# Reciprocals behind the masks, w2 jobs four units sooner, and a last token tile in two halves, in a transformer block with linear attention and a Mish MLP

## The chip, the cores and the metric

The kernel runs on one core of a Trainium2 chip. The core has five engines, each with a queue of its own that it works through in order: TensorE (PE, matmuls and transposes; its weight loads are shown as PEld), VectorE (DVE), ScalarE (ACT), GpSimd (POOL) and SyncE (SP). SP, POOL and ACT issue transfers. The engines meet at semaphores. The metric is the device time in microseconds (us) of one execution; the time of the kernel before is the median of three runs.

## The reference

One block over 2048 tokens of width 512, in float32. The six modulation vectors come from one condition vector.

```python
mod = (silu(c) @ w_mod).reshape(1, 6, 1, 512)      # sa, ca, ga, sb, cb, gb
h = layernorm(x) * (1 + ca) + sa
x = x + ga * A(h)
h = layernorm(x) * (1 + cb) + sb
x = x + gb * B(h)

def A(h):                                          # linear attention, 32 heads of 16
    q, k, v = split_heads(h @ wqkv)
    phi = lambda t: where(t > 0, t + 1, exp(t)) + 1e-6
    pq, pk = phi(q), phi(k)
    kv = einsum("bhsd,bhse->bhde", pk, v)
    z = pk.sum over tokens
    o = (pq @ kv) / ((pq * z).sum(-1) + 1e-6)
    return merge_heads(o) @ wo

def B(h):                                          # 512 -> 1792 -> 512
    t = h @ w1 + b1
    return (t * tanh(softplus(t))) @ w2
```

## The kernel before

**Numbers.** Products are made to float32 accuracy from two faster ones: every operand is split into a high part of type float32r and a low part, the rest (`split`, L71: the high part on ACT or POOL at L75 or L77, the low part on DVE at L80). A product is three matmuls (`mm3`, L65): high by high (L67), high stationary by low streaming (L68), low stationary by high streaming (L69). The stationary operand is loaded for each matmul; the streaming one has 512 columns.

**Tiling.** Tokens stand in 4 blocks of 512 (`NB`), a block in 4 tiles of 128 rows. The inner width 1792 is 14 slices of 128 (`NF`). SBUF tiles of 128x512 come from one ring of 101 slots (`sb`); a tile that is taken later waits for the last reader of the slot. PSUM has four tiles tagged "acc", three tagged "h" and one tagged "tp" (`ps`).

**Order.** The order of every engine is the order in which the Python code issues; there is no scheduler. Main loops issue PE units one after the other, and generators spawned beside them (`spawn`) are moved one step at each `tick()`, in the order in which they were spawned. A generator's step so decides behind which other instructions of DVE, ACT, POOL or SP its own will stand. An engine that waits holds up all that is behind it in its queue.

**Stages.** First the k units and, over all tokens, the sums that the attention needs (to about 107 us of the span). Then `q_unit(b, g)` makes phi(q) for block 0 and 1; `kv_ps` (L746) and two masked copies on DVE (L749, "the masks") make the block diagonal state, and four matmuls `m_ps` fold wo into it. Then come q units of blocks 2 and 3 with the output units of block 0, and then the loop over blocks 1 to 3 in which `o_unit(b, t)` number n = 4b + t (n from 4 to 13) makes one token tile of the attention's output. Output units 14 and 15 follow the first products of the MLP.

**The denominators.** `attend(b, wait, queue)` (L593) makes them for block b: 16 small matmuls into a "tp" tile (L598) and, in its next step, on DVE the addition and the reciprocal (L602, L603, the tile `rden`). They go to DRAM (L605, `rden_d`), and four loads `rd` (L609) bring them back, each head's row spread over 16 partitions. After `wait` further steps DVE multiplies the four q tiles with them (L617), and they are split (tiles `qs`). Blocks 0 to 2 use POOL's queue, block 3 SP's. Block 0's matmuls are issued just ahead of `kv_ps`, and its other steps come at the ticks behind.

**w2.** `w2_job(f)` (L499) loads a slice of w2 (L501, `w2r`, on SP's queue), after two further steps multiplies it on DVE by gb (L504), splits it (`w_0h`, `w_0l`), and stores both parts to DRAM (L510, POOL). Jobs 0 and 1 are spawned in the loop of output units, the others later, in pairs. `w2_again` (L512) loads the parts back for later blocks.

**The MLP.** For blocks 0 and 1, and 2 and 3 together, the first product is a seven-product scheme over pairs of blocks and slices: `pair_first` and `pair_unit` (L846), with products of operands `t`, `b`, `a` and `s` in "h" or "tp" tiles (`p_a`, `p_s`) and sums on DVE (L836). Output units 14 and 15 (L629 adds them to the residual and so frees their "h" tiles) stand ahead of the first `pair_unit`. `d_unit(b, f)` (L809) adds slice f of the second product for one block to four "acc" tiles, one for each token tile; at the last slice DVE adds the residual (L819) and SP stores the token tile (L820). The last block's 14 d units are the end of the program, with nothing else on PE.

Of the kernel before, what the change touches and what calls it, by code (L numbers as in the profile page):

```python
# [11 lines left out]
ALU = mybir.AluOpType  # L12

P = 128
S = 2048
D = 512
F = 1792
NB = S // 512
NF = F // P
# [6 lines left out]
def block_kernel(ctx: ExitStack, tc: tile.TileContext, x, wqkv, wo, w1, b1t, w2, c, wmodt, out):  # L26
    nc = tc.nc
    act, dve, pool, pe, sp = nc.scalar, nc.vector, nc.gpsimd, nc.tensor, nc.sync
# [9 lines left out]
    def sb(name, dt=F32, shape=(P, 512)):  # L38

        return big.tile(list(shape), dt, tag="T", name=name, bufs=SLOTS)  # L40

    def ps(tag, name, shape=(P, 512)):
        return psp.tile(list(shape), F32, tag=tag, name=name, bufs=PBUFS[tag])
# [6 lines left out]
    def spawn(gen):  # L50
        fresh.append(gen)

    def tick():

        running.extend(fresh)
        fresh.clear()
        for g in list(running):
            if next(g, "end") == "end":
                running.remove(g)

    def run(gen):
        for _ in gen:
            pass

    def mm3(o, st, mv, start, stop):  # L65

        pe.matmul(o, st[0], mv[0], start=start, stop=False)  # L67
        pe.matmul(o, st[0], mv[1], start=False, stop=False)  # L68
        pe.matmul(o, st[1], mv[0], start=False, stop=stop)  # L69

    def split(name, t, keep, key, lo_engine=dve, hi_engine=act):  # L71

        hi, lo = sb(f"{name}h", F32R, t.shape), sb(f"{name}l", F32R, t.shape)
        if hi_engine is act:
            act.activation(hi, t, AF.Copy)  # L75
        else:
            hi_engine.tensor_copy(hi, t)  # L77
        if lo_engine is dve:
            yield
        lo_engine.tensor_tensor(lo, t, f32(hi), op=ALU.subtract)  # L80
        keep[key] = hi, lo


    xt, wm, wraw = {}, {}, {}

    def load_x(b, j, key="x", eng=sp):
        t = xt[key, b, j] = sb(f"{key}_{b}_{j}")
        r0 = 512 * b + P * j
        eng.dma_start(t, x[r0:r0 + P, :])
# [194 lines left out]
    def q_unit(b, g):  # L284
        p = ps("h", f"pq_{b}_{g}")
        gs = slice(P * g, P * (g + 1))
        for k in range(4):
            mm3(p, [w[:, gs] for w in wq[k]], hT["x", b, k], k == 0, k == 3)
        pq[b, g] = sb(f"q_{b}_{g}")
        spawn(phi(p, f"q_{b}_{g}", pq[b, g]))  # L290
# [101 lines left out]
    for k in range(4):  # L392
        hi, lo = sb(f"hT_x_0_{k}h", F32R), sb(f"hT_x_0_{k}l", F32R)
# [103 lines left out]
    w2s, w2d, op_a = {}, {}, {}  # L497

    def w2_job(f, wait=2):  # L499
        t = sb(f"w2r_{f}")  # L500
        sp.dma_start(t, w2[P * f:P * (f + 1), :])  # L501
        for _ in range(wait):
            yield
        dve.tensor_tensor(t, t, bc["gb"], op=ALU.mult)  # L504
        yield
        yield from split(f"w2_{f}", t, w2s, f)
        yield
        for i in range(2):
            w2d[f, i] = drp.tile([P, D], F32R, name=f"w2d_{f}_{i}")
            pool.dma_start(w2d[f, i], w2s[f][i])  # L510
# [82 lines left out]
    def attend(b, wait, queue=pool):  # L593

        p = ps("tp", f"den_{b}")[:, 0:P]
        for g in range(4):
            for t in range(4):
                pe.matmul(p[32 * t:32 * (t + 1), :], hmask[:, g, :], pq[b, g][:, P * t:P * (t + 1)],  # L598
                          start=g == 0, stop=g == 3)
        yield  # L600
        rden = cst.tile([P, P], F32, tag="rden", name=f"rden_{b}", bufs=2)
        dve.tensor_scalar(rden, p, TINY, 1.0, op0=ALU.add, op1=ALU.mult)  # L602
        dve.reciprocal(rden, rden)  # L603
        d = drp.tile([32, 512], F32, name=f"rden_d_{b}")
        queue.dma_start(bass.AP(tensor=d.tensor, offset=d.offset, ap=[[P, 4], [512, 32], [1, P]]), rden)  # L605
        rd = []
        for g in range(4):
            r = sb(f"rd_{b}_{g}")
            queue.dma_start(r, bass.AP(tensor=d.tensor, offset=d.offset + 8 * g * 512,  # L609
                                     ap=[[512, 8], [0, 16], [1, 512]]))  # L610
            rd.append(r)
        for _ in range(wait):
            yield
        parts = []
        for g in range(4):
            t = pq[b, g]
            dve.tensor_tensor(t, t, rd[g], op=ALU.mult)  # L617
            parts.append(split(f"qs_{b}_{g}", t, qs, (b, g)))
            next(parts[-1])
            if g % 2:  # L620
                yield
                run(parts.pop(0))
                run(parts.pop(0))
# [11 lines left out]
    def o_unit(b, t, tag="acc"):  # L635
        p = ps(tag, f"o_{b}_{t}")
        ts = slice(P * t, P * (t + 1))
        for g in range(4):
            mm3(p, [q[:, ts] for q in qs[b, g]], ms[g], g == 0, g == 3)
        spawn(o_post(p, b, t))  # L640
# [52 lines left out]
    def transpose_f(b, j, ptag="tp"):  # L693
        p = ps(ptag, f"tp_n_{b}_{j}")
        for t in range(4):
            pe.transpose(p[:, P * t:P * (t + 1)], xt["n", b, t][:, P * j:P * (j + 1)], ident)  # L696
        hf[b, j] = sb(f"hf_n_{b}_{j}")
        act.activation(hf[b, j], p, AF.Identity, bias=mc[:, 12 + j:13 + j], scale=mc[:, 16 + j:17 + j])  # L698

    def split_b(b, j, name):  # L700
        return split(f"{name}_{b}_{j}", hf[b, j], op_b, (name, j % 2))

    def columns(c0, c, done):

        b11, b12, b21, b22 = [hf.pop((b, c + h)) for h in (0, 2) for b in (c0, c0 + 1)]
        t = [sb(f"t_{c0}_{c}_{i}") for i in range(4)]
        for d, u, v in (t[0], b12, b11), (t[1], b22, t[0]), (t[2], b22, b12), (t[3], b21, t[1]):
            dve.tensor_tensor(d, u, v, op=ALU.subtract)
        yield
        names = [("b11", b11), ("t2", t[1]), ("t3", t[2]), ("t1", t[0]), ("b22", b22), ("t4", t[3]), ("b21", b21)]  # L710
        halves = [split(f"{name}_{c0}_{c}", v, op_b, (name, c)) for name, v in names if name not in done]
        for n in range(0, len(halves) + 2, 2):
            for h in halves[max(n - 2, 0):n] + halves[n:n + 2]:
                next(h, None)
            yield
# [19 lines left out]
    tick()  # L735
    run(early_rows[0])
    next(early_rows[1])
    attending = attend(0, 4)
    next(attending)
    spawn(attending)  # L740
    kv_ps = ps("acc", "kv_ps")
    for g in range(4):
        for k in range(4):
# [3 lines left out]
    for j in range(2):  # L747
        js = slice(64 * j, 64 * (j + 1))
        dve.tensor_tensor(kv.rearrange("p (g m) -> p g m", g=4)[js, :, js],  # L749
                          kv_ps.rearrange("p (g m) -> p g m", g=4)[js, :, js],  # L750
                          bmask[js, js].unsqueeze(1).to_broadcast([64, 4, 64]), op=ALU.mult)
    for g in range(1, 4):
        q_unit(1, g)
        load_x(2, g, "r")
        tick()
# [24 lines left out]
    for b in range(1, NB):  # L780
        for t in range(4):
            n = 4 * b + t
            for i, j in order.get(n, ()):
                transpose_f(i, j, "h")
                spawn(split_b(i, j, f"b{j // 2 + 1}{i + 1}"))
            if n in (12, 13):
                spawn(columns(0, n - 12, ("b11", "b12", "b21", "b22")))
            if n == 14:
                break
            o_unit(b, t)  # L790
            if b == 1:
                spawn(norm_each(1, t))
            if n == 5:
                spawn(attend(3, 3, sp))
            if n in (11, 12):
                spawn(w2_job(n - 11))
            tick()


    ag = {}  # L800
# [6 lines left out]
    oacc = {}  # L807

    def d_unit(b, f):  # L809
        if f == 0:  # L810
            for t in range(4):
                oacc[t] = ps("acc", f"oacc_{b}_{t}")
        for t in range(4):
            ts = slice(P * t, P * (t + 1))
            mm3(oacc[t], [a[:, ts] for a in ag[b, f]], w2s[f], f == 0, f == NF - 1)
            if f == NF - 1:
                v = xt["r", b, t]
                r0 = 512 * b + P * t
                dve.tensor_tensor(v, oacc[t], v, op=ALU.add)  # L819
                sp.dma_start(out[r0:r0 + P, :], v)  # L820

    ub = {}

# [50 lines left out]
    def second(b, side):  # L874

        for f in range(NF):
            side(f)
            ahead(b, f + NF)
            tick()
            d_unit(b, f)  # L880
# [34 lines left out]
    def trail(f):  # L915
        if tiles:
            spawn(tiles.pop(0))
        d_unit(0, f)
        ahead(1, f)
        tick()  # L920
# [64 lines left out]
```

## Time and profile before

| what | value |
|---|---|
| median of three runs | 504.95 us (504.88 to 506.96) |
| the profiled execution's own time | 506.47 us |
| its span, first to last instruction | 504.7 us |
| PE busy | 495.5 us (98%) |
| DVE busy | 360.3 us (71%) |
| ACT busy | 257.8 us (51%) |
| POOL busy | 112.9 us (22%) |
| moved by DMA | 77.29 MB, 153 GB/s on average |

Times in the views are microseconds from the span's start. A row of the view in order of time gives start, duration, engine, line, operation, the tile written and the tiles read (buffer numbers left out, so `t_0l` stands for several tiles), the shape, and in brackets how long the engine stood idle before it and what ended that. The record of a matmul also covers its way through the array, so consecutive records overlap: what counts is the step from start to start, 0.23 us for 512 columns. "SPq" rows are the issuing of a transfer, not its duration.

### The profile page before, as it was taken

The page shows a single profiled execution, that of the slowest core. Times are in us where ns is not written, and L with a number is a line of the kernel's source. Part 1 is how long each engine was busy: PE and PEld are TensorE (multiplying, and loading weights), DVE is VectorE, ACT ScalarE, POOL GpSimd, SP SyncE. Part 2 cuts the span into 40 slices and gives each one's busy share as a digit, 9 for nine tenths or more (in the row PEclk, how much of TensorE's full clock was granted, in tenths as well). Part 3 has the DMA queues.
Part 4 walks back from the last instruction along what each step waited for, and adds up shares of the span by engine and source line. Part 5 has one row for each costly group of instructions (what it writes and reads, how often), then busy time and mean ns, then how long its engine had stood idle before and what let it go on. Part 6 is the DMA issues. An engine that isn't in the chain of part 4 may idle for free.

```text
span 504.7 us, 6900 instructions
## 1 busy us (share of the span) xinstructions
PE 495.5 (98%) x2396; PEld 404.9 (80%) x2396; DVE 360.3 (71%) x707; ACT 257.8 (51%) x463; POOL 112.9 (22%) x204
## 2 busy tenths in 40 slices
PE   7999999999999999999999999999999999999996
PEld 5778888878778888878888888888888888888885
DVE  6889785889987978986987785359886556745302
ACT  6767573523351987836677765357253344445000
POOL 3480000100212311210233345421210111470000
PEclk9999999999999999999999999999999999999999
DMA  8821503472553315372565499982842445597002
GB/s 282 303 83 44 166 21 105 153 244 72 137 111 92 88 33 161 125 228 66 157 197 188 145 297 260 348 240 87 249 130 59 125 126 155 157 338 236 32 1 83
DMA packets 52233, 77.29 MB, mean 153 GB/s; under 512 B 5805, under 2 KB 20277, under 8 KB 52198
## 3 DMA queue, kind: packets, MB, share of 16 engines
q0 software_dynamic: 19600, 37.45, 25.6%
q1 hardware_dynamic: 32452, 39.14, 24.6%
q8 instruction: 19, 0.31, 0.2%
q10 hardware_dynamic: 146, 0.26, 0.1%
q14 instruction: 16, 0.13, 0.1%
HBM read 60.83 MB, written 15.99 MB: 152 GB/s over the span
## 4 chain that ended last, share of the span: by engine, by line
PE 84%; DVE 9%; DMA 4%; issue 1%; ACT 1%; POOL 1%; DVEq 0%; POOLq 0%; ACTq 0%
PE oacc L69 10%; PE oacc L67 10%; PE oacc L68 10%; PE p_s L67 5%; PE p_s L69 5%; PE p_s L68 5%; PE p_a L67 3%; PE p_a L69 3%; PE p_a L68 3%; DMA rd<-rden_d 3%; PE gacc L68 3%; PE gacc L69 3%; PE gacc L67 3%; PE pk L69 2%; PE pk L68 2%; PE pk L67 2%
## 5 line engine op out<-in xcount | busy, mean ns | idle before, releaser
L516 POOL DMA_DIRECT2D w2b<-w2d x84 | 44.9, 538 | 102.3 <-PE p_a L69 27.0
L827 ACT ACTIVATE ub<-c,b1c 128x512 f32<-128x512 f32 x28 | 19.0, 718 | 57.5 <-DVE c L836 53.8
L836 DVE TENSOR_TENSOR u<-p_s,u 128x512 f32<-128x512 f32 x28 | 19.4, 692 | 35.2 <-PE p_s L69 25.5
L819 DVE TENSOR_TENSOR rb<-oacc,rb 128x512 f32<-128x512 f32 x8 | 5.5, 692 | 32.9 <-PE oacc L69 32.9
L836 DVE TENSOR_TENSOR u<-p_a,u 128x512 f32<-128x512 f32 x26 | 17.6, 689 | 7.5 <-PE p_a L69 6.9
L698 ACT ACTIVATE hf_n<-tp_n,mc 128x512 f32<-128x512 f32 x16 | 11.7, 771 | 19.5 <-PE tp_n L696 19.5
L189 POOL TENSOR_TENSOR rs_n<-rs_n,half 128x1 f32<-128x1 f32 x16 | 9.4, 589 | 53.9 <-DVE rs_n L215 44.3
L804 ACT ACTIVATE u<-u,b1c 128x512 f32<-128x512 f32 x26 | 18.5, 712 | 2.6 <-DVE u L836 2.6
L836 DVE TENSOR_TENSOR c<-p_s,u 128x512 f32<-128x512 f32 x28 | 18.0, 683 | 1.9 <-PE p_s L69 1.3
L241 ACT ACTIVATE e_q<-pq 128x512 f32<-128x512 f32 x16 | 9.3, 588 | 18.4 <-PE pq L69 18.4
L853 ACT ACTIVATE u<-p_a 128x512 f32<-128x512 f32 x12 | 7.1, 588 | 18.7 <-PE p_a L69 18.7
L241 ACT ACTIVATE e_k<-pk 128x512 f32<-128x512 f32 x16 | 9.4, 591 | 13.3 <-PE pk L69 13.1
L617 DVE TENSOR_TENSOR q<-q,rd 128x512 f32<-128x512 f32 x16 | 10.7, 689 | 6.9 <-DMA rd<-rden_d 6.8
L189 POOL TENSOR_TENSOR rs_x<-rs_x,half 128x1 f32<-128x1 f32 (+1 forms) x10 | 7.1, 716 | 32.1 <-DVE rs_x L184 31.3
L243 DVE TENSOR_SCALAR e_k<-e_k 128x512 f32<-128x512 f32 x16 | 6.9, 430 | 10.0 <-ACT e_k L241 9.9
L198 ACT ACTIVATE x<-x,nb_x,rs_x 128x512 f32<-128x512 f32 x15 | 11.6, 808 | 4.7 <-DVE nb_x L193 3.5
L605 POOL DMA_DIRECT2D rden_d<-rden x3 | 2.2, 738 | 45.7 <-DVE rden L603 45.7
L198 ACT ACTIVATE r<-r,nb_n,rs_n 128x512 f32<-128x512 f32 x8 | 6.5, 809 | 10.1 <-DVE nb_n L219 9.3
L244 DVE SCALAR_TENSOR_TENSOR q<-pq,e_q 128x512 f32<-128x512 f32 x16 | 11.1, 692 | 0.7
L244 DVE SCALAR_TENSOR_TENSOR ku<-pk,e_k 128x512 f32<-128x512 f32 x16 | 11.1, 692 | 0.7
L629 DVE TENSOR_TENSOR r<-o,r 128x512 f32<-128x512 f32 x16 | 10.8, 680 | 0.4 <-PE o L69 0.4
L180 DVE BATCH_NORM_STATS2 st_x<-x 128x6 f32<-128x512 f32 x13 | 8.9, 682 | 2.9 <-DMA x<-in_x_dram 2.9
(1118 smaller groups left out, 1751.9 us busy)
## 6 DMA issues: line engine op xcount, KB each, us to landing
w2b<-w2d POOLq DMA_DIRECT2D x84, 256.0 KB, 5.1
w1p<-in_w_dram SPq DMA_DIRECT2D x28, 256.0 KB, 3.1
wm<-in_wmodt_dram SPq DMA_DIRECT2D x24, 256.0 KB, 5.7
r<-in_x_dram SPq DMA_DIRECT2D x16, 256.0 KB, 2.4
x<-in_x_dram SPq DMA_DIRECT2D x15, 256.0 KB, 5.5
w2r<-in_w_dram SPq DMA_DIRECT2D x14, 256.0 KB, 3.4
rd<-rden_d POOLq DMA_DIRECT2D x12, 256.0 KB, 5.7
wr<-in_wqkv_dram SPq DMA_DIRECT2D x8, 256.0 KB, 3.2
```

The source lines that it names most:

```text
L67: pe.matmul(o, st[0], mv[0], start=start, stop=False)
L68: pe.matmul(o, st[0], mv[1], start=False, stop=False)
L69: pe.matmul(o, st[1], mv[0], start=False, stop=stop)
L189: pool.tensor_tensor(y, y, half[:, lo:hi], op=ALU.pow)
L198: act.activation(dst, t, AF.Identity, bias=nb[key, b][:, j:j + 1], scale=rs[key, b][:, j:j + 1])
L241: act.activation(e, p, AF.Exp)
L244: dve.scalar_tensor_tensor(dst, p, 0.0, e, op0=ALU.max, op1=ALU.add)
L516: pool.dma_start(w2s[f][i], w2d[f, i])
L698: act.activation(hf[b, j], p, AF.Identity, bias=mc[:, 12 + j:13 + j], scale=mc[:, 16 + j:17 + j])
L804: act.activation(u, p, AF.Mish, bias=b1c[:, f:f + 1])
L827: act.activation(u, p, AF.Mish, bias=b1c[:, f:f + 1])
L836: dve.tensor_tensor(out, p, u, op=ALU.add)
```

## The change

Three edits. First, block 0's generator of denominators gets its second step, the reciprocals and what follows them, right behind the two masked copies on DVE instead of at the next tick; one more waiting step keeps its multiplications at the same tick. Second, w2 jobs 0 and 1 are spawned beside output units 7 and 8 instead of 11 and 12. Third, in the last block the fourth token tile is made in two halves of 256 columns with PSUM tiles of their own (the fifth one tagged "h"), each half with its own addition and store; the last store is issued by ACT.

```diff
-    attending = attend(0, 4)
+    attending = attend(0, 5)
     next(attending)
-    spawn(attending)
     kv_ps = ps("acc", "kv_ps")
...
                           bmask[js, js].unsqueeze(1).to_broadcast([64, 4, 64]), op=ALU.mult)
+    next(attending)
+    spawn(attending)
     for g in range(1, 4):
         q_unit(1, g)
...
-            if n in (11, 12):
-                spawn(w2_job(n - 11))
+            if n in (7, 8):
+                spawn(w2_job(n - 7))
             tick()
...
     def d_unit(b, f):
+
+        parts = [(t, 0, D) for t in range(4)]
+        if b == NB - 1:
+            parts[3:] = [(3, 0, D // 2), (3, D // 2, D)]
         if f == 0:
-            for t in range(4):
-                oacc[t] = ps("acc", f"oacc_{b}_{t}")
-        for t in range(4):
+            for n, (t, lo, hi) in enumerate(parts):
+                oacc[n] = ps("acc" if n < 4 else "h", f"oacc_{b}_{n}")[:, 0:hi - lo]
+        for n, (t, lo, hi) in enumerate(parts):
             ts = slice(P * t, P * (t + 1))
-            mm3(oacc[t], [a[:, ts] for a in ag[b, f]], w2s[f], f == 0, f == NF - 1)
+            mm3(oacc[n], [a[:, ts] for a in ag[b, f]], [w[:, lo:hi] for w in w2s[f]], f == 0, f == NF - 1)
             if f == NF - 1:
-                v = xt["r", b, t]
+                v = xt["r", b, t][:, lo:hi]
                 r0 = 512 * b + P * t
-                dve.tensor_tensor(v, oacc[t], v, op=ALU.add)
-                sp.dma_start(out[r0:r0 + P, :], v)
+                dve.tensor_tensor(v, oacc[n], v, op=ALU.add)
+                (act if n == 4 else sp).dma_start(out[r0:r0 + P, lo:hi], v)
```

## The prediction

> **What bounds the kernel now.** I read the page first (busy shares, chain), then the busy times by stage, then the order of time around each of the three edits, and last the transfers' times to landing. Page:
>
> ```profile
> span 504.7 us, 6900 instructions
> PE 495.5 (98%) x2396; PEld 404.9 (80%) x2396; DVE 360.3 (71%) x707; ACT 257.8 (51%) x463; POOL 112.9 (22%) x204
> PE 84%; DVE 9%; DMA 4%; issue 1%; ACT 1%; POOL 1%; DVEq 0%; POOLq 0%; ACTq 0%
> ```
>
> TensorE (PE) is never idle for long: a microsecond that it waits is one at the end, and one it works less is one gained. The DVE and DMA shares of the chain lie in a few places, which the stages show (columns: stretch; busy us and count of PE, weight loads, DVE, ACT, POOL; clock; DMA share; GB/s):
>
> ```profile
> 121.00:149.00 28.00, 27.86 (x224) 20.99 (x223) 24.51 (x54) 11.86 (x24) 4.29 (x7) 1.00 0.53 124
> 149.00:172.00 23.00, 22.56 (x126) 18.07 (x126) 19.38 (x40) 9.56 (x22) 7.51 (x12) 1.00 0.37 99
> 196.00:206.00 10.00, 10.00 (x49) 8.22 (x49) 9.96 (x17) 7.10 (x12) 1.62 (x3) 1.00 0.23 92
> 206.00:219.00 13.00, 12.51 (x56) 10.02 (x54) 12.89 (x22) 7.89 (x14) 2.67 (x5) 1.00 0.67 201
> ```
>
> From 196 to 219 us DVE is busy 22.85 of 23 us: there it has no slack. Around the first edit, in order of time (start, duration, engine, line):
>
> ```profile
> 127.91 0.28 DVE L602 TENSOR_SCALAR rden<-den 128x128 f32<-128x128 f32 x1
> 128.23 0.95 DVE L603 RECIPROCAL rden<-rden 128x128 f32<-128x128 f32 x1
> 141.71 0.69 DVE L617 TENSOR_TENSOR q<-q,rd 128x512 f32<-128x512 f32 x1 [0.34 <-DMA rd<-rden_d]
> 150.57 0.63 DVE L80 TENSOR_TENSOR qs_2l<-q,qs_2h 128x512 fp32r<-128x512 f32 x1
> 150.42 0.39 PE L68 MATMUL o<-m_2l,qs_2h 128*128 128x512 f32 x1
> 151.25 0.50 PE L69 MATMUL o<-m_2h,qs_2l 128*128 128x512 f32 x1 [0.44 <-DVE qs_2l L80]
> ```
>
> The reciprocals' round trip through DRAM ends in a DVE wait, and DVE then gives qs_2l to PE too late. Around the second edit:
>
> ```profile
> 188.60 0.82 SPq L501 DMA_DIRECT2D w2r<-in_w_dram  x2
> 187.86 8.04 DMA rd<-rden_d
> 191.49 0.69 DVE L617 TENSOR_TENSOR q<-q,rd 128x512 f32<-128x512 f32 x1 [1.06 <-DMA rd<-rden_d]
> 192.10 0.69 DVE L80 TENSOR_TENSOR b_0l<-hf_n,b_0h 128x512 fp32r<-128x512 f32 x1
> 204.47 0.68 DVE L504 TENSOR_TENSOR w2r<-w2r,gb_bc 128x512 f32<-128x512 f32 x1
> 218.49 1.29 DVE L629 TENSOR_TENSOR r<-o,r 128x512 f32<-128x512 f32 x2
> 219.23 0.50 PE L67 MATMUL p_s<-t_0h,s_0h 128*128 128x512 f32 x1 [0.73 <-DVE r L629]
> DMA to landing us min/median/max: 8.6/8.6/8.6
> ```
>
> The last line is of the w2r tile alone, from 188 to 190 us. See that the two w2r loads are issued right behind the four rd loads on SP's queue, and that PE at 219.23 waits for the end of DVE's unbroken row.
>
> **The change part by part**, each against the profiled execution (span 504.7; its own time 506.47, so 1.8 us lie around the span).
>
> 1. Reciprocals behind the masks. L602 and L603 jump ahead of two wm columns, e_q and q: they start where the wm started, 125.62 instead of 127.91, 2.3 us sooner. Everything behind them on POOL (rden_d, four rd) goes 2.3 sooner; POOL waited for rden before, so nothing else on its queue is passed. What is pushed back: four DVE instructions, by 1.2 us. Of these q frees the PSUM tile that the unit of 129.97 needs; it ends at 129.2 instead of 128.0, 0.7 early still. The extra wait step of attend keeps the multiplications at their tick, so DVE's order there is unchanged. DVE reaches them at 138.56 (137.87 plus 0.69), and they ended the rd wait at 141.71: at most 2.3 us come sooner. PE's stalls they cure: 150.42 to 151.25 is 0.83 where 0.23 is the step, 0.60; 145.45 to 145.98, 0.30 (a PSUM tile freed by DVE's q at 145.24); behind each the next step is 0.34 instead of 0.23, 0.11 twice. Together 1.1. One microsecond of the 2.3 suffices, so I take all: **-1.1**. Bounds: 0 (SP's loads of 131.3 to 132.7 now compete with rd and eat the lead) and -1.1. The cover afterwards: block 1's multiplications wait at 158.26 with PE fed throughout.
>
> 2. w2 jobs four units sooner. The SP queue does not change: w2r stands behind rd in both orders and was issued at 188.6 and 189.0 already, early. POOL's four w2d stores move between x1d stores, DVE's four and ACT's two instructions forward. So the gain sought is small, since DVE's row from 192.10 to 219 holds the same instructions in another order. But the first multiplication (L504) now stands right behind the q of 191.49: DVE would begin it at 192.10. Its data is not there. The last rd lands at 187.86 + 8.04 = 195.90; the second w2r, issued at 189.0, lands 8.6 later (the one landing of the two that the trace tells), 197.6; the first lies between, and as the rds came about 2 us apart and w2r is the next in the queue I take 197.0. DVE takes its queue in order, so it stands for 4.9 us. Behind it wait b_0l, r, qs_0l and all the rest of the row. From 192.10 to 218.49 it took 26.4 us, 0.2 of them the wait for the last rd, which is now covered; the same instructions from 197.0 end at 223.2: **+4.7**. PE meets this first in the output unit of 198.71 (block 3's first): qs_0l comes at about 200.1 where 199.25 was its use, qs_2l at 204.3 where 200.62 was: stalls of about 0.9, 0.9 and 1.9. The rest it meets at 219.23, whose PSUM tile is freed by the r of 218.49, now 4.7 later. After 219 PE has no idle time that could take it up (the page shows PE full to the end). Bounds by the landing: 195.9 gives +3.6, 197.6 gives +5.3.
>
> 3. Last token tile in halves. In block 3 each of 14 units has three matmuls of 512 columns replaced by six of 256: 42 more, each with its weight load. A 512-column one steps 0.2275 us (0.23 in the rows). The eight plain f32 records of m_ps (132.69, 512 columns each, 3.60 us in all, 0.59 of it the last one's own record) step 0.43; if they pass columns at half the rate, 512 columns take 0.215 and some 0.0125 of the 0.2275 does not go with columns. A half then costs 0.120, more than the 0.109 that the 128-column transposes need with a load each (0.87 us for 8), so the load stays hidden: 42 x 0.013 = **+0.5**. Bounds: 0 (all goes with columns) and, on a straight line from 0.109 at 128 to 0.2275 at 512, 0.148 a half: 42 x 0.069 = +2.9. The Trainium skill ("TensorE: Matmul & The Clock Gate", Back-to-back issue gap) puts 262 cycles to 256 columns and 518 to 512, 6 cycles a pair; by that the term would be an estimated 0.1 us and the sum 0.4 lower. The 0.2275 measured here is above its 518 cycles, so I stay with the rows.
> At the end: the addition was 0.69 behind the last matmul; the second half's costs 0.42 (row of the 128x256 additions) but stands behind the first half's, which stands behind tile 2's, so it ends 0.67 behind instead of 0.71. The last store is half as big, on ACT's queue beside SP's: the whole ones took 2.0 us to land. I take -0.3 for it, **-0.35** in all; bounds 0 and -0.7. A fifth PSUM tile comes from "h", which nothing else uses in the last block.
>
> Sum: -1.1 + 4.7 + 0.5 - 0.35 = **+3.8**. The span would be 508.5; the profiled execution lies 1.5 above the median of the runs, so I add to the median: 504.95 + 3.8 = **508.75**.
>
> **The rivals.**
> - The forecast, 508.75. Chance 0.67.
> - w2r in time (not slower). If the first w2r lands by 192.1, part 2 is 0 and the time is 504.95 - 0.95 = 504.0; each us of landing after that adds one, and at 193.1 before and after are level. For it: SP waits on nothing but its own issue. Against: it would have to overtake the rd loads ahead of it in its queue, the last of which lands at 195.90. 0.10.
> - No gain from the reciprocals, the wait moved on to SP's competing loads: 509.85. For it: rd took 8.4 us in that traffic. Against: 1.0 of 2.3 us is enough. 0.08.
> - Halves no cheaper than wholes: 0.2275 each, 42 x 0.2275 = +9.6 instead of 0.5, 517.8. For it: no row shows a 256-column f32r matmul. Against: the transposes' 0.109 with a load. 0.06.
> - Clock lost in PE's new pauses. The first matmuls of the span step 3.65/18 = 0.203 where 128-column ones step 0.109 later, half speed for some 3 us, which costs 1.5; once more at about 204 us: 510.25. Against: the longest pause is 1.9 us, and the granted clock is 1.00 in every stage shown. The Trainium skill (same page, The HAM clock gate) lets the clock fall after an idle window of about 3.4 us; by that rule pauses of 0.9, 0.9 and 1.9 with matmuls between them would not do it, and no run here shows a pause as long. 0.09.
>
> **How the numbers follow.** About 0.5%, 2.5 us, is what a measurement of this kernel can tell from no change (its three runs spread 2.1). Inside the forecast the landing bounds give 507.65 to 509.35, the column bounds up to 2.4 more, the tail 0.35 either way. The range 506.5 to 511.3 holds the forecast, the lost gain and the clock case; out are w2r in time and the dear halves, and a part of the spread. Slower by over 0.5% (above 507.5): 0.67 less 0.05, and three rivals of 0.23, 0.85. Same: 0.12, w2r in time or nearly. Faster: 0.03.
>
> **What would show it.** DVE: L602 right behind the masks; the wait at the q of 141.71 shorter by about 2; PE's stalls at 145.98 and 151.25 gone. DVE's first w2r multiplication with some 4.9 us of idle time ended by DMA w2r, PE pauses of about 0.9, 0.9 and 1.9 at the first output unit of block 3, and the p_s of 219.23 at about 222.8 (3.6 later). In the last block matmuls of 256 columns 0.12 apart. Wrong it would be if that wait is under 1 us, or if the halves step over 0.15.

## The result

The change made the kernel slower: 511.03 us median (509.36 to 512.07, six runs) against 505.06 (504.88 to 506.96, six runs) for the kernel before beside it. The ratio over all runs is 1.0109 with a 95% interval of 1.0084 to 1.0133, which is 5.5 us (4.2 to 6.7); the two medians alone lie 6.0 us apart. The forecast was 508.75 in a range of 506.5 to 511.3: the direction held, the range held with 0.3 us to spare, and the middle was 2.3 us too low. The profiled execution of the changed kernel took 511.9 us, 1.7 of it around the span.

The page of the changed kernel, its span, its busy shares and the engines' shares of the chain that ended last:

```profile
span 510.2 us, 6981 instructions
PE 499.1 (98%) x2438; PEld 408.8 (80%) x2438; DVE 360.3 (71%) x708; ACT 257.9 (51%) x463; POOL 113.0 (22%) x204
PE 81%; DVE 9%; DMA 4%; ACT 4%; issue 2%; POOL 0%; SPq 0%; DVEq 0%; POOLq 0%; ACTq 0%
```

The page hardly tells the two kernels apart: PE is still busy 98% of the span. The stages do. The changed kernel by stage (stretch; busy us and count of PE, weight loads, DVE, ACT, POOL; granted clock; DMA share; GB/s):

```profile
121.00:149.00 28.00, 28.00 (x226) 21.41 (x225) 26.75 (x58) 12.57 (x25) 4.73 (x8) 1.00 0.46 125
149.00:172.00 23.00, 23.00 (x130) 18.76 (x129) 18.80 (x41) 10.73 (x25) 7.72 (x13) 1.00 0.40 99
196.00:206.00 10.00, 7.72 (x36) 5.55 (x35) 10.00 (x18) 6.47 (x11) 2.62 (x5) 1.00 0.30 105
206.00:224.00 18.00, 16.11 (x65) 12.79 (x64) 17.05 (x28) 8.63 (x15) 3.32 (x7) 0.91 0.44 144
```

PE has no idle time left from 121 to 172 us, where the first edit acts; how much of that is the edit's own is answered beside the third edit. From 196 to 224 us it stands for 4.2 us, and the clock of the last stretch is 0.91 on average. DVE is as full there as before. Around the first edit, the changed kernel's DVE in order of time:

```profile
125.62 0.29 DVE L602 TENSOR_SCALAR rden<-den 128x128 f32<-128x128 f32 x1
138.47 1.28 DVE L617 TENSOR_TENSOR q<-q,rd 128x512 f32<-128x512 f32 x2
148.19 0.63 DVE L80 TENSOR_TENSOR qs_2l<-q,qs_2h 128x512 fp32r<-128x512 f32 x1
```

The reciprocals start at 125.62, 2.3 us sooner, and no rd wait stands ahead of the multiplications of 138.47. qs_2l is there 2.4 us sooner, and PE's stalls at 145.98 and 151.25 are gone. By block 3's first output unit (198.71 before, 197.55 after) the kernel is 1.16 us ahead.

Around the second edit, the changed kernel in order of time:

```profile
186.65 0.88 SPq L501 DMA_DIRECT2D w2r<-in_w_dram  x2
189.85 0.69 DVE L617 TENSOR_TENSOR q<-q,rd 128x512 f32<-128x512 f32 x1 [1.24 <-DMA rd<-rden_d]
194.95 0.69 DVE L504 TENSOR_TENSOR w2r<-w2r,gb_bc 128x512 f32<-128x512 f32 x1 [4.41 <-DMA w2r<-in_w_dram]
199.97 0.50 PE L67 MATMUL o<-m_2h,qs_2h 128*128 128x512 f32 x1 [0.67 <-ACT qs_2h L75]
202.31 0.50 PE L69 MATMUL o<-m_2h,qs_2l 128*128 128x512 f32 x1 [1.61 <-DVE qs_2l L80]
213.32 0.68 DVE L841 TENSOR_TENSOR c<-p_a,u 128x512 f32<-128x512 f32 x1
214.05 0.50 PE L67 MATMUL o<-m_0h,qs_0h 128*128 128x512 f32 x1 [1.89 <-DVE c L841]
221.26 0.39 PE L67 MATMUL p_s<-t_0h,s_0h 128*128 128x512 f32 x1
```

DVE stands 4.41 us for the load of w2r, and everything behind it is late. PE then waits three times: once for ACT's qs_2h, which stands behind DVE's multiplication, and twice for DVE's own results. From start to start and beyond the step of 0.23, these pauses are 0.84 (199.97), 1.78 (202.31) and 2.05 (214.05). The third is output unit 14, whose PSUM tile (tag "h") is freed by the addition c of 213.32. After it the p_s of 221.26 does not wait at all. The landing in the changed kernel, from issue, which the trace tells for one of these two loads:

```profile
DMA to landing us min/median/max: 8.4/8.4/8.4
```

And the clock: the changed kernel in stretches of 3.41 us, the length of the one stretch in which its matmuls ran at a granted clock of 0.50 (columns as above):

```profile
198.18:201.59 3.41, 1.85 (x7) 0.89 (x6) 3.41 (x7) 2.31 (x5) 0.12 (x1) 1.00 0.20 77
...
211.83:215.24 3.41, 1.52 (x7) 1.01 (x6) 3.41 (x7) 2.21 (x4) 0.54 (x1) 1.00 0.32 86
215.24:218.65 3.41, 3.41 (x10) 2.64 (x9) 3.27 (x6) 2.95 (x6) 0.00 (x0) 0.50 0.46 149
```

From 215.24 to 218.65 the granted clock is 0.50. There the matmuls step 0.43 us instead of 0.23:

```profile
216.22 0.63 PE L68 MATMUL o<-m_2l,qs_2h 128*128 128x512 f32 x1
216.65 0.63 PE L69 MATMUL o<-m_2h,qs_2l 128*128 128x512 f32 x1
```

Half of 3.41 us is lost by that, 1.7. The six runs agree: four with a mean clock of 0.995 took 510.9 to 512.1 us, two with 0.998 and 0.999 took 509.4 and 509.7.

### The profile page after: what moved, and what is told of

Its sections match the earlier page's. It is cut to its first block, busy times and chain, and to the rows that moved or that the text cites. A ratio compares the mean times of both kernels' runs of the same rounds, so it can differ in the third digit from the quotient of the medians.

```text
span 510.2 us, 6981 instructions
## 1 busy us (share of the span) xinstructions
PE 499.1 (98%) x2438; PEld 408.8 (80%) x2438; DVE 360.3 (71%) x708; ACT 257.9 (51%) x463; POOL 113.0 (22%) x204
## 4 chain that ended last, share of the span: by engine, by line
PE 81%; DVE 9%; DMA 4%; ACT 4%; issue 2%; POOL 0%; SPq 0%; DVEq 0%; POOLq 0%; ACTq 0%
PE oacc L68 10%; PE oacc L69 10%; PE oacc L67 10%; PE p_s L69 5%; PE p_s L68 5%; PE p_s L67 5%; PE p_a L69 3%; PE p_a L68 3%; PE p_a L67 3%; PE gacc L68 3%; PE gacc L69 3%; PE gacc L67 2%; PE pk L69 2%; PE pk L68 2%; PE pk L67 2%; PE pq L67 2%
## 5 line engine op out<-in xcount | busy, mean ns | idle before, releaser
L824 DVE TENSOR_TENSOR rb<-oacc,rb 128x512 f32<-128x512 f32 (+1 forms) x9 | 5.5, 630 | 33.7 <-PE oacc L69 33.7
L504 DVE TENSOR_TENSOR w2r<-w2r,gb_bc 128x512 f32<-128x512 f32 x14 | 9.1, 685 | 4.4 <-DMA w2r<-in_w_dram 4.4
```

## The experiments

Two theories stood at the start. Late transfer: the multiplications were moved to where their data is not there yet, and DVE's wait for it is the loss, with the clock's fall as its follow-up. Order: the two multiplications themselves, 0.69 us each, push back what PE needs, whatever the load does. The first four kernels also take the three edits apart.

| kernel | median us | lowest to highest | runs | ratio to before, 95% |
|---|---|---|---|---|
| the change | 511.03 | 509.36 to 512.07 | 6 | 1.0109 (1.0084 to 1.0133) |
| reciprocals alone | 504.95 | 504.71 to 506.19 | 12 | 0.9980 (0.9967 to 0.9994) |
| w2 jobs alone | 510.53 | 509.00 to 512.22 | 6 | 1.0091 (1.0065 to 1.0117) |
| halves alone | 506.67 | 505.72 to 509.17 | 12 | 1.0014 (0.9993 to 1.0035) |
| change, w2r loaded early | 505.58 | 505.01 to 507.06 | 12 | 0.9994 (0.9980 to 1.0007) |
| change, pauses filled | 509.37 | 509.20 to 511.02 | 6 | 1.0071 (1.0050 to 1.0092) |
| reciprocals, w2 jobs seven units sooner | 504.50 | 504.23 to 504.99 | 11 | 0.9970 (0.9957 to 0.9983) |
| change, w2r loaded early, no halves | 504.45 | 504.15 to 505.84 | 11 | 0.9972 (0.9960 to 0.9984) |

The kernel before had a median of 506.35 beside the first four experiments (29 runs, 504.76 to 509.19) and 505.92 beside the last three (23 runs, 504.60 to 508.04), so ratios count here, and medians within a group.

### The first edit alone

```diff
-    attending = attend(0, 4)
+    attending = attend(0, 5)
     next(attending)
-    spawn(attending)
...
+    next(attending)
+    spawn(attending)
     for g in range(1, 4):
```

> The kernel before with the first edit alone (the reciprocals right behind the masks). Theory: the two stalls of the tensor engine at 145.98 and 151.25 go, 1.1 us off, about 504.0 against 505.1, and no wait on rd in the vector engine's row of block 0. Rival (the gain is lost again further on, in the long wait at the p_s of 219.23, which is set by the vector engine's full row and not by what comes before): the first stage is 1.1 us shorter but the p_s wait grows from 0.73 to about 1.8, and the time stays at 505.1.

Measured 0.9980, which is 1.0 us less (0.3 to 1.7). PE of this kernel, in order of time:

```profile
150.06 0.39 PE L68 MATMUL o<-m_2l,qs_2h 128*128 128x512 f32 x1
150.29 0.39 PE L69 MATMUL o<-m_2h,qs_2l 128*128 128x512 f32 x1
217.58 0.50 PE L67 MATMUL p_s<-t_0h,s_0h 128*128 128x512 f32 x1 [0.16 <-DVE r L629]
```

The step from 150.06 to 150.29 is the plain 0.23, and the p_s waits 0.16 where it waited 0.73: the rival, by which that wait would grow, falls. But the fastest run of this kernel (504.71) is no faster than the fastest of the kernel before (504.76). What goes is the upper end, 506.19 against 509.19. The experiment on the halves tells why.

### The second edit alone

```diff
-            if n in (11, 12):
-                spawn(w2_job(n - 11))
+            if n in (7, 8):
+                spawn(w2_job(n - 7))
```

> The kernel before with the second edit alone (the first two w2 jobs four units sooner). Theory (late transfer): the first w2r multiplication waits for its load 4.4 to 4.9 us, as in the changed kernel's trace, and the tensor engine loses 3.9 us by waiting for what stands behind it: 509.0 if the granted clock stays at 1.00, about 510.9 if it falls to half for 2 us after the pauses. Rival (the load is late only because the first edit moved the rd loads): no wait, 505.1.

Measured 1.0091, 4.6 us more (3.3 to 5.9). This kernel in order of time:

```profile
194.93 0.69 DVE L504 TENSOR_TENSOR w2r<-w2r,gb_bc 128x512 f32<-128x512 f32 x1 [4.25 <-DMA w2r<-in_w_dram]
199.94 0.50 PE L67 MATMUL o<-m_2h,qs_2h 128*128 128x512 f32 x1 [0.42 <-ACT qs_2h L75]
202.29 0.50 PE L69 MATMUL o<-m_2h,qs_2l 128*128 128x512 f32 x1 [1.61 <-DVE qs_2l L80]
214.03 0.50 PE L67 MATMUL o<-m_0h,qs_0h 128*128 128x512 f32 x1 [0.30 <-DVE c L836]
```

The wait is there without the first edit, so the rival falls. In this execution the clock fell one pause sooner; its stretches of 3.41 us:

```profile
199.51:202.92 3.41, 1.38 (x6) 0.82 (x6) 3.41 (x7) 3.41 (x7) 0.99 (x2) 1.00 0.00 1
202.92:206.33 3.41, 3.41 (x12) 2.77 (x11) 3.41 (x6) 2.81 (x5) 1.41 (x4) 0.50 0.69 231
```

Here the 1.7 us were lost ahead of the pause of output unit 14, and that pause shrank from 2.05 to 0.47: the unit starts at 214.03 here and at 214.05 in the changed kernel, because DVE's c decides in both. So here the lost clock cost nothing, because PE would have waited behind it anyway; behind the last pause, as in the changed kernel, it cost its full price.

### The third edit alone

```diff
+        parts = [(t, 0, D) for t in range(4)]
+        if b == NB - 1:
+            parts[3:] = [(3, 0, D // 2), (3, D // 2, D)]
...
+                (act if n == 4 else sp).dma_start(out[r0:r0 + P, lo:hi], v)
```

> The kernel before with the third edit alone (last token tile in two halves of 256 columns in block 3). Theory of the prediction: +0.5 for 42 more matmuls at 0.120 us a half, -0.35 at the end, 505.2 in all. As the changed kernel's trace reads: +0.65 for the matmuls and only -0.05 at the end, because the two half stores lie among the whole ones on the same 16 DMA engines: 505.65. Rival (the fifth PSUM tile from the group h costs a wait, or the halves keep the weight loads from hiding): over 506.

Measured 1.0014 (0.9993 to 1.0035), which is 0.7 us more with zero inside the interval; the clean measure of the halves is the last experiment's. The median of 506.67 lies over the 506 of the rival, but the base of this group is 506.35, and the rows of the last block show none of the rival's waits. PE of this kernel at its end, in order of time:

```profile
496.73 0.28 PE L67 MATMUL oacc<-w2b,a_12h 128*128 128x256 f32 x1
496.85 0.28 PE L68 MATMUL oacc<-w2b,a_12h 128*128 128x256 f32 x1
496.97 0.28 PE L69 MATMUL oacc<-w2b,a_12l 128*128 128x256 f32 x1
497.09 0.40 PE L67 MATMUL oacc<-w2b,a_13h 128*128 128x512 f32 x1
497.32 0.40 PE L68 MATMUL oacc<-w2b,a_13h 128*128 128x512 f32 x1
497.56 0.39 PE L69 MATMUL oacc<-w2b,a_13l 128*128 128x512 f32 x1
```

A half steps 0.12; the block's first of a unit, behind a whole one, 0.11, and the mean is 0.1188. The whole ones right behind the halves step 0.233, 0.236 and 0.228, where before every one of the block stepped 0.2267. Over the block's 126 whole ones the mean is 0.2295.

This kernel issues the reciprocals as the kernel before does, and it answers what the first edit is worth. Its row in block 0's multiplications and PE's step behind it:

```profile
140.29 1.29 DVE L617 TENSOR_TENSOR q<-q,rd 128x512 f32<-128x512 f32 x2 [1.59 <-DMA rd<-rden_d]
149.74 0.63 DVE L80 TENSOR_TENSOR qs_2l<-q,qs_2h 128x512 fp32r<-128x512 f32 x1
150.42 0.50 PE L69 MATMUL o<-m_2h,qs_2l 128*128 128x512 f32 x1
```

DVE waits 1.59 for rd, once, and qs_2l comes at 149.74, 0.8 sooner than in the profiled execution of the kernel before, where it waited twice, 2.46 in all. The longer of those two waits stands ahead of the q of 141.71:

```profile
140.68 0.69 DVE L617 TENSOR_TENSOR q<-q,rd 128x512 f32<-128x512 f32 x1 [2.12 <-DMA rd<-rden_d]
```

PE steps 0.30 instead of 0.83. The kernel with the second edit alone reads the same (one wait of 1.63). So the stalls of 1.1 us in the profile of before belong to an execution in which rd landed late; with the same order of reciprocals they can be missing. Block 3's first output unit starts at 197.89 here, at 197.90 with the second edit alone and at 197.62 with the first edit alone, so where rd is not late the first edit is worth about 0.3 us.

### The change with w2r loaded early

```diff
+    w2r = {}
+
+    def w2_load(f):
+        w2r[f] = sb(f"w2r_{f}")
+        sp.dma_start(w2r[f], w2[P * f:P * (f + 1), :])
...
+            if n in (4, 5):
+                w2_load(n - 4)
             if n in (7, 8):
                 spawn(w2_job(n - 7))
```

> The changed kernel with one thing moved: the two w2r loads are issued at steps 4 and 5 of block 3's loop, ahead of the four rd loads on SP's queue; the multiplications stay where the change has them, and the vector engine's order is the same. Theory (late transfer): the data is there, the 4.41 us wait at the first multiplication is gone, the tensor engine's pauses at 199.97, 202.31 and 214.05 with it, the clock stays at 1.00, and the time is 505.06 - 1.16 + 0.65 = 504.5 or up to 1 us less, where the p_s wait of 0.73 goes too. Rival (the order itself: two multiplications of 0.69 us put ahead of b_0l, r and qs_0l make these late): pauses at the first output unit of about 1.4 us in all stay, and the time is about 506. Rival (the rd loads, now behind w2r on the queue, come later by the 2 x 2 us of w2r's transfer): the wait moves to the q of 191.49, which waits 3 to 4 us more, and the time stays near 508 or over.

Measured 505.58, a ratio of 0.9994 (0.9980 to 1.0007), against 1.0109 for the change. DVE of this kernel, and below it the landing of its first two w2r loads:

```profile
189.25 0.69 DVE L624 TENSOR_TENSOR q<-q,rd 128x512 f32<-128x512 f32 x1 [0.54 <-DMA rd<-rden_d]
189.86 0.68 DVE L511 TENSOR_TENSOR w2r<-w2r,gb_bc 128x512 f32<-128x512 f32 x1
```

```profile
DMA to landing us min/median/max: 2.5/2.6/2.6
```

Issued at 159.4 and 162.7 us, some 25 us sooner and ahead of the rd loads, the same transfers land in 2.6 us instead of 8.4. How much of that is the place in the queue and how much the other traffic of that time (92 GB/s from 158 to 166 us, 133 from 183 to 197 in the changed kernel) was not separated. The multiplication runs at 189.86 with no wait, and all three pauses are gone: PE is busy without a gap from 196 to 224 us. DVE's order is that of the change, so the order theory falls, and so does the rival of a later rd (0.54 us of waiting, not 3 to 4). The theory's 504.5 was 0.6 under its base of 505.06; against the base of this group the ratio gives 0.3 less (1.0 less to 0.4 more), which agrees within the noise. Two of its terms are off all the same: the halves cost more than the +0.65 in it, as the last experiment shows, and the -1.16 in it is more than the first edit gives a median run.

### The change with the pauses filled

```diff
+    def fill(n):
+        w = ps("tp", "fill")
+        for i in range(n):
+            pe.transpose(w[:, 0:P], ident, ident)
...
+            if (b, t, g) == (3, 0, 2):
+                st, mv = [q[:, ts] for q in qs[b, g]], ms[g]
+                fill(6)
+                pe.matmul(p, st[0], mv[0], start=False, stop=False)
+                pe.matmul(p, st[0], mv[1], start=False, stop=False)
+                fill(14)
+                pe.matmul(p, st[1], mv[0], start=False, stop=False)
+                continue
...
+        if t == 2:
+            fill(16)
         o_unit(NB - 1, t, "h")
```

> The changed kernel with throw-away transposes put into the tensor engine's three new pauses (6 ahead of qs_2h's and 14 ahead of qs_2l's matmuls of block 3's first output unit, 16 ahead of output unit 14; 36 x 0.109 = 3.9 us of work where the pauses were 0.84, 1.78 and 2.05). The waits stay as they are; only the idle time is filled. Theory (the clock falls because of the idle time: the granted clock goes to 0.50 for 3.41 us where a stretch of that length had over 2 us of idle time): the clock stays at 1.00 through 198 to 220 us in every run, the profile shows no stretch at 0.50, and the median falls by up to 1.7 us, to about 509.4, with the spread of 509.4 to 512.1 gone. Rival (the clock falls for another reason, such as the load after the pause): stretch at 0.50 and median 511 as before. Rival (the transposes delay the matmuls behind them): 511 to 512 with the clock at 1.00.

Measured 509.37, a ratio of 1.0071 (1.0050 to 1.0092) against 1.0109 (1.0084 to 1.0133) for the change, with more work on PE. The two intervals overlap a little; the clock tells more. The stretches of this kernel:

```profile
200.33:203.74 3.41, 3.31 (x23) 2.58 (x22) 3.41 (x7) 3.41 (x7) 1.03 (x2) 1.00 0.00 0
211.83:215.24 3.41, 3.25 (x23) 2.76 (x22) 3.41 (x6) 1.72 (x4) 0.54 (x1) 1.00 0.27 92
215.24:218.65 3.41, 3.41 (x17) 2.80 (x16) 3.27 (x7) 3.35 (x7) 0.00 (x0) 1.00 0.64 207
```

The clock stays at 1.00, and the mean clock was 0.998 or more in all six runs, where the change had 0.995 in four of six. The waits are the same and only the idle time is gone, so the idle time was the cause. Part of the theory missed: two of the six runs still took 510.8 and 511.0. The profile is of the latter:

```profile
195.71 0.69 DVE L504 TENSOR_TENSOR w2r<-w2r,gb_bc 128x512 f32<-128x512 f32 x1 [4.53 <-DMA w2r<-in_w_dram]
214.81 0.50 PE L67 MATMUL o<-m_0h,qs_0h 128*128 128x512 f32 x1 [0.16 <-DVE c L854]
```

There the load landed 0.8 us later than in the profile of the change, and output unit 14 began 0.8 later. So in this execution the later transfer accounts for the longer time, with the clock at 1.00.

### Two versions that move the load as well

The first keeps the w2 jobs whole and spawns them at steps 4 and 5, on top of the first edit:

```diff
-            if n in (11, 12):
-                spawn(w2_job(n - 11))
+            if n in (4, 5):
+                spawn(w2_job(n - 4))
```

> The kernel before with the first edit, and the first two w2 jobs spawned at steps 4 and 5 of block 3's loop, seven units sooner than before: load ahead of the rd loads, multiplications ahead of the vector engine's full row. No halves. Theory: the loads are there, the multiplications take idle time of the vector engine from before 192 us, the full row ends 1.4 us sooner and the p_s wait goes: 0.45 us under the first edit alone, about 504.5 against 505.0 with it. Rival (the rd loads come too late behind 2 x 256 KB on SP's queue): a wait on rd of over 1.5 us at the first q of block 3, and the time above that of the first edit alone.

Measured 504.50, a ratio of 0.9970 (0.9957 to 0.9983) against 0.9980 (0.9967 to 0.9994) for the first edit alone. The 0.45 us of the theory do not stand clear of the noise, and the profiled executions have spans of 503.2 and 503.1. DVE of this kernel in block 3, and below it PE at output unit 14:

```profile
180.15 0.68 DVE L504 TENSOR_TENSOR w2r<-w2r,gb_bc 128x512 f32<-128x512 f32 x1
183.75 0.68 DVE L504 TENSOR_TENSOR w2r<-w2r,gb_bc 128x512 f32<-128x512 f32 x1
191.57 0.69 DVE L617 TENSOR_TENSOR q<-q,rd 128x512 f32<-128x512 f32 x1 [2.20 <-DMA rd<-rden_d]
```

```profile
209.47 0.50 PE L67 MATMUL o<-m_0h,qs_0h 128*128 128x512 f32 x1 [0.21 <-DVE c L837]
```

Both multiplications lie ahead of the full row, and the p_s wait is gone, as the theory said. The rd wait grew to 2.20, as the rival said, yet the time did not rise. In this trace PE waits at output unit 14 instead of at the p_s, and the two come out level.

The second is the change with the early load and d_unit as it was before.

> The changed kernel with the early loads of the w2r tiles and without the third edit. Against the same kernel with the halves (505.58 median) this gives the cost of the third edit by itself. As the traces read (84 half matmuls at 0.1188 us for 42 whole ones at 0.2267: +0.46; the whole ones right behind the halves at 0.228 to 0.236: +0.35; the end +0.07): 0.9 less, about 504.7. Rival (the halves' smaller last store pays at the end as the prediction had it, +0.5 - 0.35): 0.15 less, 505.4.

Measured 504.45 against 505.58 with the halves: they cost 1.1 us by the medians, which come from two groups. The two traces, the sharper measure, say 0.83 (spans of 503.48 and 502.65): 0.45 for the halves themselves (84 x 0.1187 less 42 x 0.2267), 0.36 for the whole ones behind them (126 x 0.0029) and 0.06 from the end of the last matmul to the end of the span, less 0.04 by which the block with halves began sooner. The rival, with a gain at the end, falls. By its stages PE of this kernel has no gap:

```profile
196.00:206.00 10.00, 10.00 (x50) 8.25 (x49) 9.86 (x17) 7.28 (x13) 3.74 (x7) 1.00 0.48 161
206.00:224.00 18.00, 18.00 (x81) 14.92 (x80) 16.98 (x30) 9.17 (x16) 1.62 (x3) 1.00 0.52 159
```

The span of 502.65 is 0.4 under that of the first edit alone, where the p_s still waited. Both versions beat the kernel before, by 0.30% (0.17 to 0.43) and 0.28% (0.16 to 0.40), and by the ratios they are 1.4% faster than the change. Most of what they gain on the kernel before is the first edit's (0.20%).

## Why the prediction was right, and where it was not

- **Reciprocals, -1.1.** The row was read rightly and the size is about right: -1.0 (0.3 to 1.7), and 1.16 us between the two profiled executions. What was wrong is the base. The sum was made against an execution 1.5 us above the median and added to the median, with the words that the profiled execution lies 1.5 above. About 0.9 of those 1.5 us were the very stalls that the edit removes, and most of the rest a longer p_s wait: the two traces with the old order and no late rd lack both. For a run at the median of 504.95 this term should have been nearer zero, about -0.3 by those traces. That every slow run of the kernel before is slow by a late rd is argued from three traces, not shown run by run. The sign to look for named the q of 141.71, whose own wait is 0.34; the wait that mattered was the 2.12 ahead of it.
- **w2 jobs, +4.7.** The mechanism was right: the load behind four rd loads, DVE's queue in order, PE waiting for qs_2h and qs_2l. The first landing was put at 197.0 and came at 194.93. The rd loads ahead of it were issued 1.9 us sooner than before, and DVE was ready for it at 190.54 instead of 192.10, so the wait of 4.9 came out as 4.41. The first three pauses were foreseen as 0.9, 0.9 and 1.9; there were 0.1 (qs_0l), 0.84 and 1.78. The rest was put at the wrong place. It was to be met at the p_s of 219.23, at about 222.8; it was met at output unit 14, 7 us sooner, which needs a PSUM tile that DVE's c frees, and the p_s of 221.26 ran on without a pause. The amount hardly differs: with all pauses and the slow steps behind them, and less the p_s wait that went, PE waits 4.1 us more than before. That it came near although the place was wrong is in part luck; nothing in the prediction tied it to output unit 14.
- **The clock, a rival with +1.5 and a chance of 0.09.** It happened: 3.41 us at 0.50, 1.7 us lost, in four of six runs by their mean clock. This is the step that failed, and it is most of the 2.3 us by which the forecast was low. The argument against it was that the longest pause is 1.9 us and that the Trainium skill ("TensorE: Matmul & The Clock Gate", The HAM clock gate) lets the clock fall after an idle window of about 3.4 us. Two of the three pauses that were foreseen came about as long as said, the first hardly at all, and in the profiled execution they left the clock at 1.00. It fell behind a fourth, ahead of output unit 14, of which 1.89 us lay in one stretch of 3.41 us; the sum had no pause there. With the w2 jobs alone two of the foreseen pauses, 0.42 and 1.61 us of idle time in one such stretch, were enough. So the argument failed on both its legs: neither the longest pause nor a whole idle window decides. The other rivals fall: DVE waited 4.41 us for w2r, no rd wait stood ahead of block 0's multiplications, and a half steps 0.1188.
- **Halves, +0.5.** 0.45 measured for the half matmuls, at 0.1187 where 0.120 was taken. The estimate of 0.1 from the Trainium skill's issue gap (same page, Back-to-back issue gap) was too low here. Left out was the cost to the neighbours: the nine whole matmuls behind each unit's six halves take 0.026 us longer in all, 0.36 over the block.
- **The end, -0.35.** Not found. From the end of the last matmul to the end of the span the halves are 0.06 slower. The last half store, issued by ACT at 506.70 in the changed kernel, landed 2.15 us later; the whole one before took 2.05. The four stores ahead of it keep the DMA engines busy back to back (DMA share 0.98 from 505.5 to 508.0), and a smaller last one does not get ahead of them.

Put together on the span of the profiled execution, with the terms as the traces have them: 504.7 - 1.16 + 4.1 + 1.7 + 0.8 is 510.1; the span of the changed kernel is 510.2.

## What to carry to other kernels

Before an instruction is moved forward in an in-order queue, look up when its operands land, not when they were issued: the same load landed 8.4 us after its issue behind four others, and 2.6 when it was issued some 25 us sooner, ahead of them; moving the load as well took the whole loss of the move away. A profiled execution above the median can contain the very wait that an edit removes, so the gain must not be taken off the median in full. And when PE gets new pauses, add up the idle time that can fall into one stretch of 3.41 us: a single pause of 1.89 us put the clock down in the changed kernel, and two of 0.42 and 1.61 together with the w2 jobs alone.

## What the runs showed of the hardware

- The clock went down although PE was never idle for longer than about 2 us at a stretch. Both times the stretch at 0.50 lasted 3.41 us (215.24 to 218.65; 202.92 to 206.33), and it began a whole multiple of 3.413 us after the point at which the trace's record of the full clock starts (7.03 to 215.24 is 61 of them, 4.94 to 202.92 is 58). That fits the free-running window of 3.413 us that the Trainium skill describes ("TensorE: Matmul & The Clock Gate", The HAM clock gate). It does not fit the same section's rule that the clock falls after an idle window: here windows in which PE was busy for 1.52 and 1.38 of 3.41 us were enough, while one with 1.85 was not. Where the point lies stays open. In the kernel with w2r loaded early and no halves the last matmuls end inside such a window, and the next one is still at 1.00; the trace's record falls to 0.50 only one window later, at 503.83:

```profile
497.00:500.42 3.42, 1.51 (x7) 0.93 (x5) 2.24 (x4) 0.00 (x0) 0.00 (x0) 1.00 0.68 260
500.42:502.65 2.23, 0.00 (x0) 0.00 (x0) 0.00 (x0) 0.00 (x0) 0.00 (x0) 1.00 0.18 72
```

  Here 1.51 us busy were enough to hold the clock, where 1.52 were not in the changed kernel: the records also cover a matmul's way through the array, and do not tell the two apart. The 1.90 us of idle time in this window are one piece, longer than either of the 0.42 and 1.61 that brought the clock down with the w2 jobs alone, so the longest pause does not decide. That the loss differs from run to run because the pauses fall differently among the windows fits this, but was not shown run by run.
- Lost clock ahead of a pause cost nothing here. In the kernel with the w2 jobs alone PE lost its 1.7 us at 203 to 206 and reached output unit 14 at 214.03, as in the changed kernel (214.05), which had lost none by then.
- A matmul of 256 columns costs 0.1188 us and makes the whole ones behind it dearer, 0.228 to 0.236 against 0.2267, for about five of them.
